# Block-causal attention with a two-stage expert MLP on one Trainium2 core: scores of query blocks 0 to 3 as two rounded full-array products per head

## The chip, the cores and the metric

The kernel runs on one core of one Trainium2 chip. The metric is the device time of one execution in microseconds. The kernel before takes 956.35 us, the median of three runs (955.95 to 956.46).

## What is computed

Attention with a mask by blocks of 64 tokens, then a dense MLP with an ELU between its two matrices, then a soft mixture of eight small experts. Inputs are float32: 8 batches, 8 heads, 576 tokens, head size 64; 4608 tokens of width 512 after attention.

```python
scores = scale * np.matmul(q, k.transpose(0, 1, 3, 2))
scores = np.where(block_i >= block_j, scores, -1000000000.0)
attn = softmax(scores); x = np.matmul(attn, v)      # then (B*S, H*D)
h = x @ w_in; g = np.where(h > 0, h, np.exp(np.minimum(h, 0)) - 1)
x = g @ w_out
logits = x @ phi                                    # 32 slots, 8 experts
slot_out = experts(softmax(logits, 0).T @ x)        # relu(. @ w1[e]) @ w2[e]
return softmax(logits, 1) @ slot_out
```

## The kernel before

**Work and stages.** Two heads of one batch are a pair; there are 32 pairs (`n` = 0 to 31), and 36 tiles of 128 tokens for the MLP. Attention of a batch runs ahead of the tiles that need it, so that from about 200 us to 757 us of the span both run side by side: one pair and 1.125 tiles in some 24 us. Then come the last tiles, then the tail with the experts, whose 32 MB of weights are read in part while the tiles still run.

**Order.** No loop runs on the chip. Each step is entered in a `Plan` with its engines, an assumed duration, what it reads and writes, and a key (a due time); `Plan.order` plays the steps through with those durations and writes the order of every engine. An engine then works through its list strictly in order, so a step that is not ready holds all that stand behind it on that engine. TensorE's steps carry a mode: F (the array as one 128 by 128 block), R (two halves of 64 rows), C (column halves), D (four blocks of 32 columns), and the plan charges 0.13 for a change between them.

**One pair.** `pair_load` brings q and k; `pair_prep` makes q and k transposed (head size on partitions, head 0 on 0 to 63, head 1 on 64 to 127). Pairs 0 to 7 (`n < NTP`) load rows and turn them on TensorE (L360) with ScalarE copies (L521). From pair 8 on, blocks of 32 are loaded and turned by VectorE (L525), and GpSimd scales q (L528, L531). RQ, RK, QT and KT have two buffers each, by `n % 2`. `pair_scores` has four fills: fill 0 is the last half block of queries (block 4, 64 rows, from pair 8 on as a full-array product, L568); fills 1, 2 and 3 are query block 3, blocks 2 and 0, and block 1, for both heads (L576). These are plain float32 products over 64 rows, the two heads on the two halves of the array. Each unit then gets its mask (VectorE memset, L584), its maximum (VectorE, L587) and its exponential with sum (ScalarE, L590). `pair_weights` normalises on GpSimd (L607), turns the result (VectorE L689 and a DRAM round trip `swapped`, TensorE L360 for some blocks), and `swapped_values` multiplies with v (L739, mode C).

**One tile.** `tile_split` rounds x to a high part on ScalarE (L793) and takes the rest on GpSimd (L795). Then, for four ranges of 512 columns, twelve rounded products (L808 to L810, mode F) fill one of two PSUM banks, ScalarE takes the exponential (L813), VectorE clips it (L815, SBUF to SBUF) and takes the maximum with the bank (L818), which frees the bank for the range after next. The result is turned by VectorE (L826) and a DRAM round trip (`turned`); the routing products (L853, L919, mode D) follow, with L880 and L881 between.

**DMA.** Nearly all transfers are issued by SyncE (SP), in one list (L355).

## Time and profile before

| | |
|---|---|
| median of three runs | 956.35 us (955.95 to 956.46) |
| profiled execution, its own time | 955.77 us |
| its span, first to last instruction | 954.0 us |
| TensorE busy / VectorE / ScalarE / GpSimd | 908.7 / 675.9 / 439.4 / 272.6 us |
| granted TensorE clock, mean | 0.99 |

Busy time is what the profiler saw as running; matmuls overlap in it, so that TensorE's real pace is read from the chain of work (each step from the end of the one before), not from the mean length of an instruction. Two records stand for one float32 product and one for a rounded product, so "L576 x4" is two products.

### The profile page before, as it was taken

What the parts mean: (1) busy time and instruction counts of PE and PEld (TensorE: products, weight loads), DVE (VectorE), ACT (ScalarE), POOL (GpSimd) and SP (SyncE); (2) the same over time, 40 slices, a digit from 0 to 9 for tenths busy, and PEclk for the clock granted to TensorE, in tenths of its full rate; (3) what the DMA queues carried; (4) which work ended last, traced back from release to release, by engine and by line L of the source; (5) the groups of instructions that cost most, each with busy time, mean ns of one, the idle gap of its engine ahead of it and who ended that gap; (6) DMA issues with size and microseconds to landing.
All of it is one profiled execution on the core that took longest, in us unless ns stands there. A gap on an engine that the chain in (4) does not pass through costs nothing.

```text
span 954.0 us, 19403 instructions
## 1 busy us (share of the span) xinstructions
PE 908.7 (95%) x6708; PEld 623.3 (65%) x6708; DVE 675.9 (71%) x1718; ACT 439.4 (46%) x1285; POOL 272.6 (29%) x428
## 2 busy tenths in 40 slices
PE   8889999999999999999999999999999999999992
PEld 6556777666666766676766666766776776766350
DVE  5887795668787887777888878887887844333160
ACT  5775655445445535444445445444444333322143
POOL 2863442133342332222323432332332210000000
PEclk9999999999999999999999999999999999999996
DMA  9846755647777785767677777667756498068969
GB/s 235 243 130 171 220 184 159 146 115 207 202 203 218 197 209 184 212 181 211 194 203 206 199 208 201 202 188 203 206 163 217 144 305 340 3 216 298 377 223 342
DMA packets 253217, 197.08 MB, mean 207 GB/s; under 512 B 183232, under 2 KB 206400, under 8 KB 250048
## 3 DMA queue, kind: packets, MB, share of 16 engines
q1 hardware_dynamic: 251920, 195.55, 69.1%
q8 instruction: 54, 0.88, 0.4%
q10 hardware_dynamic: 1200, 0.30, 0.1%
q14 instruction: 43, 0.35, 0.1%
HBM read 125.52 MB, written 70.25 MB: 205 GB/s over the span
## 4 chain that ended last, share of the span: by engine, by line
PE 74%; DVE 8%; DMA 7%; SPq 4%; ACT 2%; issue 2%; POOL 1%; ACTq 0%; DVEq 0%; POOLq 0%
PE ps L808 13%; PE ps L810 11%; PE ps L809 11%; PE ps L360 8%; PE ps L576 7%; PE ps L739 7%; SPq L355 4%; PE ps L919 3%; PE ps L568 2%; PE ps L853 2%; DMA att<-swapped 2%; DMA swapped<-att 2%; PE ps L767 2%; DVE base L587 2%; PE ps L460 1%
## 5 line engine op out<-in xcount | busy, mean ns | idle before, releaser
L808 PE MATMUL ps<-w,xhl 128*128 128x512 f32 x576 | 249.8, 434 | 7.8 <-DVE g L818 5.5
L607 POOL TENSOR_SCALAR att<-att,base 128x128 f32<-128x128 f32 (+4 forms) x288 | 181.0, 647 | 222.2 <-DVE base L603 151.0
L810 PE MATMUL ps<-w,xhl 128*128 128x512 f32 x576 | 226.8, 394 | 0.0
L809 PE MATMUL ps<-w,xhl 128*128 128x512 f32 x576 | 225.7, 392 | 0.0
L590 ACT ACTIVATE att<-ps,base 128x128 f32<-128x128 f32 (+4 forms) x288 | 157.4, 552 | 122.9 <-DVE base L587 121.0
L587 DVE TENSOR_REDUCE base<-ps 128x1 f32<-128x128 f32 (+4 forms) x288 | 135.7, 503 | 21.3 <-PE ps L572 12.2
L808 PEld LDWEIGHTS ps<-w,xhl 128*128 128x128 f32 x576 | 108.8, 189 | 52.0 <-issue 19.1
L813 ACT ACTIVATE xe<-ps 128x512 f32<-128x512 f32 x144 | 86.0, 600 | 115.0 <-PE ps L810 113.7
L810 PEld LDWEIGHTS ps<-w,xhl 128*128 128x128 f32 x576 | 108.1, 188 | 24.9
L336 ACT COPY att<-ps 128x128 f32<-128x128 f32 (+3 forms) x192 | 75.7, 434 | 95.8 <-PE ps L360 90.6
L809 PEld LDWEIGHTS ps<-w,xhl 128*128 128x128 f32 x576 | 108.9, 189 | 14.8
L815 DVE TENSOR_SCALAR xe<-xe 128x512 f32<-128x512 f32 x144 | 68.1, 473 | 67.0 <-ACT xe L813 65.6
L576 PE MATMUL ps<-att 64*128 64x128 f32 (+3 forms) x512 | 96.1, 468 | 1.0 <-ACT att L590 1.0
L360 PE MATMUL ps<-base,att 128*128 128x128 f32 (+1 forms) x496 | 83.2, 282 | 9.7 <-POOL att L607 8.5
L360 PEld LDWEIGHTS ps<-base,att 128*128 128x128 f32 (+1 forms) x496 | 58.0, 143 | 44.5 <-POOL att L607 17.6
L795 POOL TENSOR_TENSOR xhl<-xe,xhl 128x512 fp32r<-128x512 f32 x36 | 46.3, 1291 | 133.1 <-ACT xhl L793 127.0
L818 DVE TENSOR_TENSOR g<-xe,ps 128x512 f32<-128x512 f32 x108 | 73.3, 680 | 2.4
L689 DVE STREAM_TRANSPOSE att<-att 128x384 f32<-128x384 f32 x144 | 70.4, 507 | 5.3 <-POOL att L607 4.2
L739 PE MATMUL ps<-att 128*64 128x64 f32 (+4 forms) x864 | 71.9, 318 | 1.2 <-DMA att<-swapped 0.7
L576 PEld LDWEIGHTS ps<-att 64*128 64x128 f32 x512 | 42.0, 185 | 40.6 <-issue 14.1
L739 PEld LDWEIGHTS ps<-att 128*64 128x64 f32 x864 | 46.8, 137 | 32.3 <-issue 23.6
L826 DVE STREAM_TRANSPOSE g<-g 128x512 f32<-128x512 f32 x84 | 58.0, 695 | 1.7 <-DMA turned<-g 0.2
(134 smaller groups left out, 1115.1 us busy)
## 6 DMA issues: line engine op xcount, KB each, us to landing
turned<-g SPq DMA_DIRECT2D x60, 512.0 KB, 3.1
swapped<-att SPq DMA_DIRECT2D x24, 1024.0 KB, 4.6
g<-turned SPq DMA_DIRECT2D x120, 96.0 KB, 2.6
att<-in_moe_w_dram SPq DMA_DIRECT2D x11, 1024.0 KB, 11.8
att<-swapped SPq DMA_DIRECT2D x48, 192.0 KB, 3.9
att<-in_v_dram SPq DMA_DIRECT2D x64, 128.0 KB, 3.2
g<-in_moe_w_in_dram SPq DMA_DIRECT2D x16, 512.0 KB, 5.3
w_late<-in_moe_w_dram SPq DMA_DIRECT2D x8, 1024.0 KB, 6.9
```

What stands on the lines that cost most here:

```text
L336: nc.scalar.copy(o, i)
L360: mm(o, lhsT=i, rhs=f(IDN + base, n, base, base + n), start=True, stop=True, is_transpose=True)
L576: mm(pb(at((u, h)), P * (u + 1)), lhsT=f(qt + P * u, P, 64 * h, 64 * h + 64), rhs=f(kt, P * (u + 1), 64 * h, 64 * h + 64), start=True, sto ...
L587: add("DVE", 0.08 + wide(x) / 960, lambda e, x=x, c=c: nc.vector.tensor_reduce(out=f(c, 1), in_=pb(at(x), wide(x)), axis=AX.X, op=ALU.max, ...
L590: add("ACT", 0.50 + wide(x) / 1300, lambda e, x=x, c=c: nc.scalar.activation(f(pat(x, n), wide(x)), pb(at(x), wide(x)), AF.Exp, bias=f(c, ...
L607: add("POOL", (0.28 + wide(x) / 1050) * (1.3 if n < 8 else 1.0), lambda e, x=x, p=p: nc.gpsimd.tensor_scalar(out=f(p, wide(x)), in0=f(p, w ...
L739: mm(pb(o, w, 64 * h, 64 * h + 64), lhsT=f(vs + 320 * h + D * c, D), rhs=rhs(h), start=start, stop=stop)
L808: mm(pb(bank, 512), lhsT=fr(xh + P * kk, P), rhs=hi, start=(kk == 0), stop=False)
L809: mm(pb(bank, 512), lhsT=fr(xh + P * kk, P), rhs=lo, start=False, stop=False)
L810: mm(pb(bank, 512), lhsT=fr(xl + P * kk, P), rhs=hi, start=False, stop=(kk == 3))
L813: add("ACT", 0.48, lambda e: nc.scalar.activation(f(ee, 512), pb(bank, 512), AF.Exp), r=[("h", hb)], w=[("e", hb)], key=kr)
L818: add("DVE", 0.6, lambda e: nc.vector.tensor_tensor(out=f(g, 512), in0=f(ee, 512), in1=pb(bank, 512), op=ALU.max), r=[("e", hb), ("h", hb) ...
```

## The change

Pairs 9 to 31 (`n >= STACK`, 23 pairs) compute fills 1 to 3 in another way; pair 8 goes over to the load and preparation of pairs 0 to 7. For a head, q is rounded (`X1`, ScalarE) and its difference taken (`X2`, GpSimd); k likewise (`Y`, `KL`). The rounded q is copied by DMA to the other 64 partitions, and k's difference goes by DMA below the rounded k, so that `X1` holds the high part twice, `Y` the high over the low part, and `X2` the low part over zeros. Two rounded products over all 128 rows, `X1` by `Y` and `X2` by `Y`, are added up in PSUM: high by high, high by low, low by high. `RQ`, `RK`, `QT`, `KT` and the stacks have one buffer for these pairs; q and k of a pair are loaded once the buffer is free, and `pair_prep` is entered behind the scores of the pair before. The masks of fill 2 are two memsets and not four. In the tail, one of the 1 MB weight slots comes in four transfers.

```diff
+TLAG, LATE, NTP, JOINED, STACK = 2.5, 30, 8, 5, 9
-    RQ = aa.take(2 * S)
-    RK = aa.take(2 * S)
-    QT = aa.take(2 * S)
-    KT = aa.take(2 * S)
+    RQ, QB = PT + 8 * XW + 4 * YW, PT + 8 * XW + 4 * YW + S
+    RK = aa.take(S)
+    QT = (aa.take(S), qa.take(S))
+    KT = (aa.take(S), qa.take(S))
...
+    def pair_split(n, key):
+        add("POOL", 0.64, lambda e: nc.gpsimd.tensor_scalar(
+            out=f(QT[0], 512), in0=f(QT[0], 512), scalar1=SCALE, scalar2=0.0, op0=ALU.mult, op1=ALU.add), w=[("qt", 0)], key=key + 0.5)
+        for h in range(2):
+            here, there = (D * h, D * h + D), (D - D * h, P - D * h)
+            x1, x2, y, kl = X1[h], X2[h], Y[h], KL
+            add("ACT", 0.5, lambda e, x1=x1, here=here: nc.scalar.copy(st(x1, 512, *here), f(QT[0], 512, *here)),
+                r=[("qt", 0)], w=key_of(0), key=key + 1)
+            add("ACT", 0.5, lambda e, y=y, here=here: nc.scalar.copy(st(y, 512, *here), f(KT[0], 512, *here)),
+                r=[("kt", 0)], w=key_of(1), key=key + 1)
+            load(lambda x1=x1, there=there: st(x1, 512, *there, F32), lambda x1=x1, here=here: st(x1, 512, *here, F32), 200000,
+                 r=key_of(0), w=key_of(2), key=key + 2, lag=TLAG)
+            add("POOL", 1.35, lambda e, y=y, here=here: nc.gpsimd.tensor_tensor(
+                out=st(KL, 512, *here), in0=f(KT[0], 512, *here), in1=st(y, 512, *here, F32), op=ALU.subtract),
+                r=[("kt", 0)] + key_of(1), w=[("kl", h)], key=key + 2)
+            load(lambda y=y, there=there: st(y, 512, *there, F32), lambda here=here: st(KL, 512, *here, F32), 200000,
+                 r=[("kl", h)], w=key_of(3), key=key + 3, lag=TLAG)
+            add("POOL", 1.47, lambda e, x1=x1, x2=x2, here=here: nc.gpsimd.tensor_tensor(
+                out=st(x2, 512, *here), in0=f(QT[0], 512, *here), in1=st(x1, 512, *here, F32), op=ALU.subtract),
+                r=[("qt", 0)] + key_of(0), w=key_of(4), key=key + 3)
...
+        if n >= STACK and not last:
+            for h in range(2):
+                mine = [u for u, y in units if y == h]
+                def st_sc(e, h=h, mine=mine):
+                    for u in mine:
+                        for x, first in ((X1, True), (X2, False)):
+                            mm(pb(at((u, h)), P * (u + 1)), lhsT=st(x[h] + P * u, P), rhs=st(Y[h], P * (u + 1)), start=first, stop=not first)
+                add("PE", sum(2 * (0.016 + P * (u + 1) / 2400) for u in mine), st_sc, r=[("stack", h, j) for j in range(6)], w=[bkeys[h]], key=key)
...
-        ev.append((base - (27 if n < NTP else KLD), lambda n=n, x=base - KLD: pair_load(n, x)))
-        ev.append((base - 14, lambda n=n, x=base - 14: pair_prep(n, x)))
+        ev.append((base - (27 if n < STACK else KLD) if n < STACK else max(base - KLD, free + 0.1), lambda n=n, x=base - KLD: pair_load(n, x)))
+        ev.append((before + 12.1 if n >= STACK else base - 14, lambda n=n, x=base - 14: pair_prep(n, x)))
```

The plan writes all lists anew. The next fence shows TensorE's list at fill 2 of pair 15 (L576 scores, L808 to L810 the tile's products) before:

```order
L808 MATMUL ps<-w_69,xhl 128x512
L809 MATMUL ps<-w_69,xhl 128x512
L810 MATMUL ps<-w_69,xhl 128x512
L576 MATMUL ps<-att 128x384 x2
L576 MATMUL ps<-att 128x128 x2
L808 MATMUL ps<-w_69,xhl 128x512
L809 MATMUL ps<-w_69,xhl 128x512
L810 MATMUL ps<-w_69,xhl 128x512
```

and now, at the same fill, where L620 is the stacked scores, L854 to L856 the tile's products, L899 and L965 routing, L926 and L927 what were L880 and L881:

```order
L899 MATMUL ps<-g,base 32x128 x16
L965 MATMUL ps<-att,base 32x512 x4
L854 MATMUL ps<-w_71,xhl 128x512
L855 MATMUL ps<-w_71,xhl 128x512
L856 MATMUL ps<-w_71,xhl 128x512
L620 MATMUL ps<-qk_late_2028 128x384 x2
L620 MATMUL ps<-qk_late_2028 128x128 x2
L926 MATMUL ps<-base 128x128
L927 MATMUL ps<-base 128x32
L620 MATMUL ps<-qk_late_2028 128x384 x2
L620 MATMUL ps<-qk_late_2028 128x128 x2
L854 MATMUL ps<-w_68,xhl 128x512
```

The scores now stand in the mode of the work around them, with twice the products, one head after the other, and other work may stand between the heads.

GpSimd's list between two preparations of q (L528 and L531), at pair 15, before:

```order
L528 TENSOR_SCALAR base<-att 64x64 x2
L531 TENSOR_SCALAR att<-att 128x512
L607 TENSOR_SCALAR att<-att,base 128x384 x2
L607 TENSOR_SCALAR att<-att,base 128x128 x2
L607 TENSOR_SCALAR att<-att,base 128x256 x2
L795 TENSOR_TENSOR xhl<-xe,xhl 128x512
L607 TENSOR_SCALAR att<-att,base 128x576
L607 TENSOR_SCALAR att<-att,base 128x512 x2
```

and now (L534 and L546 prepare q, L653 normalises, L841 is the tile's difference, L565 and L560 are the differences of q and k):

```order
L534 TENSOR_SCALAR att<-att 64x64 x2
L546 TENSOR_SCALAR att<-att 128x512
L653 TENSOR_SCALAR att<-att,base 128x576
L653 TENSOR_SCALAR att<-att,base 128x512 x2
L565 TENSOR_TENSOR qk_late_2028<-att,qk_late_2028 64x512
L560 TENSOR_TENSOR qk_late_2028<-att,qk_late_2028 64x512 x2
L565 TENSOR_TENSOR qk_late_2028<-att,qk_late_2028 64x512
L653 TENSOR_SCALAR att<-att,base 128x384 x2
L653 TENSOR_SCALAR att<-att,base 128x128 x2
L653 TENSOR_SCALAR att<-att,base 128x256 x2
L841 TENSOR_TENSOR xhl<-xe,xhl 128x512
```

Four differences in a row now stand ahead of the second half of the normalising.

## Rows read from the trace of the kernel before

**Rows 1.** The page, busy time and share of each engine.
```profile
PE 908.7 (95%) x6708; PEld 623.3 (65%) x6708; DVE 675.9 (71%) x1718; ACT 439.4 (46%) x1285; POOL 272.6 (29%) x428
```
**Rows 2.** Stretch: length; busy us of PE, PEld, DVE, ACT, POOL; granted clock; DMA.
```profile
200.00:757.00 557.00, 547.96 (x3934) 379.42 (x3933) 452.33 (x1200) 258.56 (x826) 177.31 (x303) 1.00 0.70 196
```
**Rows 3.** Waits of TensorE from 200 to 757 us: us, times, longest.
```profile
PE ps L808 <- DVE g L818: 5.5, 6, 2.0
PE ps L808 <- DVE att L818: 2.2, 3, 1.0
```
**Rows 4.** Waits of SP's queue, whole span.
```profile
SPq L1001 <- POOL xhl L795: 40.3, 1, 40.3
```
**Rows 5.** Chain of work in order of time: start us, us, what (records).
```profile
412.21 1.06 PE ps L576 x4
...
415.57 0.23 PE ps L809
...
416.73 0.22 PE ps L880 x2
416.95 0.14 PE ps L881 x2
417.09 1.07 PE ps L576 x8
418.16 0.43 PE ps L808
```
**Rows 6.** The same view at other places of the span.
```profile
163.34 1.12 PE ps L572 x8
...
320.87 0.44 PE ps L360 x4
...
428.63 0.97 PE ps L568 x4
429.61 0.23 PE ps L808
...
450.91 0.63 PE ps L576 x4
451.54 0.59 PE ps L360 x4
```
**Rows 7.** Groups: busy us, mean ns, idle; L795 and L815 from 200 to 757.
```profile
L795 POOL TENSOR_TENSOR xhl<-xe,xhl 128x512 fp32r<-128x512 f32 x27 | 34.7, 1288 | 60.1 <-ACT xhl L793 54.0 <-PE ps L360 6.1
L815 DVE TENSOR_SCALAR xe<-xe 128x512 f32<-128x512 f32 x104 | 49.7, 478 | 24.0 <-ACT xe L813 22.7
L441 ACT CAST w<-g 128x512 fp32r<-128x512 f32 x12 | 7.2, 624 | 1.3 <-DVE g L431 1.3
```
**Rows 8.** DMA issues: count, KB each, median us to landing.
```profile
att<-in_v_dram SPq DMA_DIRECT2D x64, 128.0 KB, 3.2
```
**Rows 9.** Timeline of SP's queue: start us, us, what.
```profile
410.75 2.06 SPq L355 DMA_DIRECT2D att<-in_k_dram  x4
```
**Rows 10.** Lines L815 and L818: duration ns min/median/max.
```profile
L815 DVE TENSOR_SCALAR xe<-xe x144: 373/427/1236, 89.8 to 867.2; 128x512 f32<-128x512 f32 x144
L818 DVE TENSOR_TENSOR g<-xe,ps x108: 643/687/690, 90.7 to 867.6; 128x512 f32<-128x512 f32 x108
```
**Rows 11.** Timelines of GpSimd, VectorE and TensorE: start, us, what, [idle before <-releaser].
```profile
212.64 1.04 DVE L815 TENSOR_SCALAR xe<-xe 128x512 f32<-128x512 f32 x1
...
214.51 0.50 PE L808 MATMUL ps<-w,xhl 128*128 128x512 f32 x1 [1.97 <-DVE g L818]
...
274.12 1.29 POOL L795 TENSOR_TENSOR xhl<-xe,xhl 128x512 fp32r<-128x512 f32 x1 [2.37 <-ACT xhl L793]
...
274.45 1.24 DVE L815 TENSOR_SCALAR xe<-xe 128x512 f32<-128x512 f32 x1
...
276.47 0.50 PE L808 MATMUL ps<-w,xhl 128*128 128x512 f32 x1 [0.85 <-DVE g L818]
...
691.98 0.64 DVE L815 TENSOR_SCALAR xe<-xe 128x512 f32<-128x512 f32 x1 [0.41 <-ACT xe L813]
```

More of the change, by code (lines that the diff above doesn't have):

```diff
@@ L258, in attention_moe_kernel @@
     SM = base.take(144)
-    QB = base.take(2 * P)
     XR = xe.take(4 * RING)
@@ L280, in attention_moe_kernel @@
     PB = aa.take(2 * PW[0] + PW[1])
+    X1, X2, Y, KL = (0, 512), (1024, 1536), (2048, 2560), 3072
+    qa.take(KL + 512 - qa.size)
     XH = xa.take(2 * 512)
@@ L321, in pb, with st @@
         return ps[p0:p1, o:o + n]
+    def st(x, n, p0=0, p1=P, dtype=F32R):
+        t = renew("qk", F32R)
+        return (t if dtype == F32R else t.bitcast(F32))[p0:p1, x:x + n]
     H0, GTB, POST, SB0, PTB, PVB = 0, 1024, 1536, 2048, 3072, 3584
@@ L531, in pair_prep @@
-        add("POOL", 0.55, lambda e: nc.gpsimd.tensor_scalar(
-            out=f(QT + S * s, 512), in0=f(QT + S * s, 512), scalar1=SCALE, scalar2=0.0, op0=ALU.mult, op1=ALU.add),
-            w=[("qt", s)], key=key + 1)
+                out=f(QB + P * s + D * h, D, D * h, D * h + D), in0=f(QT[0] + 512, D, D * h, D * h + D),
+                scalar1=SCALE, scalar2=0.0, op0=ALU.mult, op1=ALU.add), r=[("qt", 0)], w=[("qb", s, h)], key=key + 3.5)
+        if n == STACK:
+            handover([("stack", h, j) for h in range(2) for j in range(6)], [("qt", 1), ("kt", 1)] + [("raw", x, h) for x in range(3) for h in range(3)])
+            for h in range(2):
+                add("POOL", 0.4, lambda e, h=h: nc.gpsimd.memset(st(X2[h], 512, D - D * h, P - D * h, F32), 0.0), w=[("stack", h, 5)], key=key - 20)
@@ L553, in pair_scores @@
         s = n % 2
-        qt, kt = QT + S * s, KT + S * s
+        one = s if n < STACK else 0
+        qt, kt = QT[one], KT[one]
         banks, bkeys = ((H0, H0 + 512), [("h", 0), ("h", 1)]) if n < 4 and fill % 2 else ((SB0, SB0 + 512), [("sb", 0), ("sb", 1)])
@@ L564, in sc @@
         def sc(e):
-            if fill == 0 and n >= NTP:
+            if fill == 0 and n >= STACK:
                 for y in range(2):
@@ L578, in pair_scores @@
         cols = S if fill == 0 else sum(wide(x) for x in units) // 2
-        last = fill == 0 and n >= NTP
-        add("PE", (0.0 if last else 0.15) + cols / 600, sc, r=([("qb", s, 0), ("qb", s, 1)] if last else [("qt", s)]) + [("kt", s)], w=bkeys, key=key,
-            load=1.0, mode="F" if last else "R")
+        last = fill == 0 and n >= STACK
+        if n >= STACK and not last:
+            for h in range(2):
+                mine = [u for u, y in units if y == h]
[4 more added lines that the diff above has]
+                add("PE", sum(2 * (0.016 + P * (u + 1) / 2400) for u in mine), st_sc, r=[("stack", h, j) for j in range(6)], w=[bkeys[h]], key=key)
+        else:
+            add("PE", (0.0 if last else 0.15) + cols / 600, sc, r=([("qb", s, h) for h in range(3)] if last else [("qt", one)]) + [("kt", one)],
+                w=bkeys, key=key, load=1.0, mode="F" if last else "R")
         for x in units:
-            if x != "b":
+            if n >= STACK and fill == 2 and x[0] == 2:
+                both = pb(at(x) + 256, 256, 0, 64).rearrange("p (a y) -> p a y", a=2)[:, :, 64:]
+                add("DVE", 0.14, lambda e, both=both: nc.vector.memset(both, MASKED), w=keys(x), key=key)
+            elif x != "b" and not (n >= STACK and fill == 2):
                 add("DVE", 0.11, lambda e, x=x: nc.vector.memset(pb(at(x) + P * x[0] + 64, 64, 0, 64), MASKED), w=keys(x), key=key)
@@ L985, in tail, with __getitem__ @@
         wslot = [(held("w%d" % r, j), wk[r]) for r in range(4) for j in range(2)]
-        slots = [(flat(PT + PIECE * j), att) for j in range(10)]
+        class Parted:
+            def __getitem__(self, at):
+                c = at[1]
+                t = renew("qk", F32, 1)[:, PIECE + 512 * c:PIECE + 512 * c + 512] if c < 3 else f(PT + 8 * PIECE, 512)
+                return t
+        parted = Parted()
+        slots = [(flat(PT + PIECE * j), att) for j in range(8)]
+        slots += [(lambda: renew("qk", F32, 1)[:, 0:PIECE].rearrange("p (c d) -> p c d", d=512), qkk), (lambda: parted, qkk + att)]
         slots += [(flat(TT), tgk(0, 0) + tgk(0, 1))]
@@ L1000, in fn @@
                 o = at()
-                nc.sync.dma_start(out=o.rearrange("p (c f) d -> p c (f d)", f=2) if wide else o,
-                                  in_=src.rearrange("(c p) d -> p c d", p=P))
-            add("SP", 0.48, fn, r, pkeys(j), kp, 1 << 20)
+                if o is not parted:
+                    nc.sync.dma_start(out=o.rearrange("p (c f) d -> p c (f d)", f=2) if wide else o,
+                                      in_=src.rearrange("(c p) d -> p c d", p=P))
+                    return
+                for c in range(4):
+                    part = src[P * (c // 2):P * (c // 2) + P, 512 * (c % 2):512 * (c % 2) + 512] if wide else src[P * c:P * c + P, :]
+                    nc.sync.dma_start(out=o[:, c, :], in_=part)
+            add("SP", 0.48 if j != 9 else 1.9, fn, r, pkeys(j), kp, 1 << 20)
             return at, j
@@ L1177, in attention_moe_kernel @@
     ev = []
+    before = None
     for n in range(NPAIR):
```

50 lines of the change are left out of this document (27 added, 23 removed).

## Prediction

> **What bounds the kernel now.** I read the page first: TensorE is busy for 95% of the span, VectorE for 71% [rows 1]. An average over stages can mislead, so the next view is the stretch that the change touches, 200 to 757 us, in which pairs and tiles run side by side. There TensorE is busy for 548.0 of 557.0 us at the full clock (1.00, that is 2.4 GHz), VectorE for 452.3, GpSimd for 177.3 [rows 2]. So 9 us of TensorE's time are open, and its waits say whose they are: 5.5 and 2.2 us before a tile's first product L808, until VectorE's L818 has freed the PSUM bank [rows 3]. TensorE's own list of work bounds this stretch; VectorE is second. What TensorE saves here comes off the end nearly in full, as long as no new wait takes its place. The tail shifts as a whole: SP's queue stands 40.3 us before the tail's weights because slots are still held by the last tiles [rows 4], so an earlier end of the tiles lets the weights start earlier by as much.
>
> The sum is made against the profiled execution: 954.0 us of span, 955.8 of its own time, 0.6 below the median of the runs.
>
> **The products.** Pace is read from the chain. Fills 1, 2 and 3 now take 1.06, 1.07 and 0.63 us [rows 5, 6]; 23 pairs make 23 x 2.76 = 63.5 us. After the change a pair has 16 rounded products: four each of 512, 384, 256 and 128 columns. A rounded full-array product of 512 columns takes 0.23 in the chain (L809) [rows 5]. For narrow ones two rows bound the pace: L881, only 32 columns wide but with full weight loads, takes 0.14 for two records, 0.07 each [rows 5], and a 128-column transpose takes 0.44 for four, 0.11 each [rows 6]. I take 0.23, 0.18, 0.12 and 0.08: 4 x 0.61 = 2.44 us a pair, 56.1 in all, a gain of **7.4 us**. With plain proportion to the width it is 2.30 (gain 10.6), with 0.11 at the narrow end 2.56 (gain 4.6). So the gain on the products alone is small.
>
> **The changes of mode.** The other half is what follows a half-array block. L808 right behind L576 takes 0.43 [rows 5], behind L568 0.23 [rows 6]; four transposes behind L576 take 0.59, else 0.44 [rows 6]. A return to the whole array costs 0.15 to 0.20 us, taken as 0.19. In TensorE's list I counted the returns from modes R, C and D to F: 150 before (87 from R, 15 from C, 48 from D), 107 now (28, 25, 54). A part of what R gave up is paid by C and D blocks that used to share a return with R. So 43 x 0.19 = **8.2 us**. The entry into R is inside the 63.5 already.
>
> **Pair 8** goes back to ten transposes on TensorE (10 x 0.11 = 1.1) and its fill 0 from 0.97 to 1.12 plus a return [rows 6]: **1.5 us** against. Its four ScalarE copies lie beside other work.
>
> TensorE's list is thus shorter by 7.4 + 8.2 - 1.5 = **14.1 us** (11 to 17.5 with the bounds above).
>
> **What hides the rest, and what if not.** Per pair, ScalarE gets four casts, at most 0.62 us each (L441, on twice the partitions) [rows 7], GpSimd four differences at some 1.29 (L795) [rows 7], SP four issues of some 0.5 [rows 9]. In sum 57, 119 and 46 us, against 298, 380 and much of SP's time free in the stretch [rows 2]; taken at nothing as sums. VectorE loses two memsets a pair, and pair 8's two transposes: at nothing too, a gain of 1 us at the most, since VectorE's stalls are 7.7 us in all [rows 3]. Three places are not covered by sums.
>
> First, **GpSimd against VectorE**. At 274.12 a tile's difference L795 starts on GpSimd and runs to 275.41; L815 starts on VectorE at 274.45 and takes 1.24 us, to 275.69, where its median is 0.427 and its maximum 1.236; L818 follows, and TensorE's L808 waits 0.85 [rows 10, 11]. The same stands at 212.64, before the longest wait of the stretch, 1.97 [rows 11]. Of the 27 L795 in the stretch [rows 7], six lie over the start of an L815 (first 212.64, second 274.45, last 691.98 [rows 11]); these six lose 2.6 us together, of which I trace 1.8 to waits of TensorE (0.6 of the 1.97, 0.8 of the 0.85, and 0.4 at two short waits of L880 for VectorE). The change adds 92 instructions of L795's kind: 92 x 1.8 / 27 = **6.1 us** lost. Below: nothing, if they fall where L815 does not stand on the path. Above: 104 L815 in 557 us [rows 7] and 119 us of differences give 22 meetings; at the worst one seen, 0.81 us, and all of it passed on, 18 us. The value taken is nearest to the rows, being the same instruction by count.
> The Trainium skill's page "SBUF — State Buffer", section "Who interferes with whom", states that GpSimd shares one port pair with VectorE as an exclusive lock, and that a VectorE `tensor_scalar` in a two-port mode waits until a running GpSimd instruction has ended. By that rule the mean wait would be half of 1.29, 0.65 us, and 22 x 0.65 = 14 us of VectorE time, if every meeting holds. The trace agrees with the lock at 274.45, and with the other side of the Trainium skill's rule too, that an instruction with one SBUF and one PSUM input goes free: L818 stays within 643 to 690 ns [rows 10].
>
> Second, **the stack comes late**. With one buffer, nothing of the next pair's stack can be written before fill 3 of the pair is done. Then four casts (the first must end before a difference starts), three differences up to the second head's k, an issue and a 128 KB transfer (v's takes 3.2 us [rows 8]): 0.62 + 3 x 1.29 + 0.5 + 3.2 = 8.2 us. In the new list I added up TensorE's work between fill 3 and the next fill 1 with the chain's durations: 22 gaps, mostly 9.3 to 13.3 us, three short ones of 6.0, 7.1 and 7.8. The first head's fill 1 (0.46) may run first, so 1.7 and 0.6: **2.3 us** lost. At nothing if the chain is under 6.5 us; the upper end is a rival below. Queued behind a late transfer on SP are the `turned` loads that feed the routing products, and behind the differences on GpSimd the second half of the normalising.
>
> Third, ScalarE has four casts, 2.5 us, ahead of the exponential L813 of the bank that was just filled. The two banks cover 12 x 0.23 = 2.8 us, and L813, L815 and L818 need about 1.7; the cover is 1.1. I take nothing, with 5 us (0.2 a pair) as the upper end.
>
> **Sum.** 955.8 - 14.1 + 6.1 + 2.3 = 950.1; plus 0.6 to the median, 950.7. Forecast **950.7 us**.
>
> **The rivals.** (a) *The gain comes whole.* The meetings fall where VectorE has room, and the stack is early. For it: three short gaps only, and most of TensorE's gaps exceed 9 us. Against it: two of the longest waits already come from such meetings. 956.35 - 14.1 = 942; with the upper end of the products 939. (b) *GpSimd's lock eats it all.* A new wait of L808 for L818 takes the place of what was saved: 13 to 16 us, that is most of the 22 meetings at 0.65 us passed on; 955 to 958. For it speaks the lock as the Trainium skill states it (SBUF page, above); against it that the six meetings of before passed on two thirds of 2.6 us, and that tiles mostly have other work between two ranges. (c) *Slower: the stack is late at fill 1.* Place: TensorE at L620 with 512 columns, in order, so everything behind it stands. With the 22 gaps, a chain of 9.5 us costs 8 us, of 10.5 us 13, of 11 us 17, of 12 us 29. With the lock's 6.1 paid, it decides from about 9.5 us on: only 1.3 over my 8.2, which holds no hops and no queueing. At 11 us the time is 956.35 - 14.1 + 6.1 + 17 = 965. Against it: the transfer lies inside the core and may land in less than v's 3.2, and later waits overlap with it. (d) *The change does not do what it says*: rounded products are paced by their weight loads at 0.19 or more whatever the width, 73.6 us for 23 pairs, a loss of 10 where 7.4 were gained; 968. L881 at 0.07 a record speaks against it.
>
> **How the numbers follow.** Forecast 0.48 (own range 946 to 954.4), (a) 0.23, (b) 0.12, (c) 0.13, (d) 0.04. What a measurement of this kernel can tell from no change is about 0.2%, 954.4 to 958.3. Faster: the forecast and (a), 0.71; same: (b), 0.12; slower: (c) and (d), 0.17. The range goes from 940, inside (a), to 962, the lighter half of (c).
>
> **What would show it.** In the changed profile: L620 at 0.23, 0.18, 0.12, 0.08 in the chain, and L854 behind it at 0.23; TensorE's list shorter by about 14 us; waits of L854 for VectorE's L864 of some 14 us where 7.7 stood, with L861 long under an L560 or L565; waits of L620 for a DMA or GpSimd of 2 to 3 us, at three pairs. The forecast is wrong if L620 waits at most pairs, if narrow L620 take 0.19, or if TensorE's waits stay at 9 us (then a).

## The result: slower by 1.4%

The changed kernel takes 969.13 us (median; 966.05 to 970.76), the kernel before 956.15 in the runs beside it: ratio 1.0138, 95% interval 1.0105 to 1.0170. The forecast was 950.7 with a range of 940 to 962, so it missed the side and the range. The profiled execution of the changed kernel took 968.08 us, its span is 966.3. One of the four executions of a later run, e2, took 2224 us and is left out of its time.

| | before | after |
|---|---|---|
| median, us | 956.15 | 969.13 |
| span of the profiled execution, us | 954.0 | 966.3 |
| whole span: TensorE busy / idle, us | 908.7 / 45.3 | 908.3 / 58.0 |
| 200 to 757 us: TensorE busy / open, us | 547.96 / 9.0 | 536.48 / 20.5 |
| the same: VectorE, ScalarE, GpSimd busy, us | 452, 259, 177 | 461, 314, 295 |
| the same: granted clock, DMA share | 1.00, 0.70 | 0.99, 0.79 |

"Open" is the stretch of 557 us less TensorE's busy time, "idle" the same of the whole span. The stretch has the same length in every kernel, so a slower kernel gets less of its work done in it, and its busy and open time mirror each other; how long the work itself takes is read from the whole span, in which every kernel does all of it. First the page's busy times of the changed kernel and the row of the stretch (length; busy us of PE, PEld, DVE, ACT, POOL; granted clock; DMA share; GB/s); they answer to [rows 1, 2].

```profile
PE 908.3 (94%) x6721; PEld 654.2 (68%) x6721; DVE 687.5 (71%) x1656; ACT 501.4 (52%) x1396; POOL 390.3 (40%) x519
...
200.00:757.00 557.00, 536.48 (x3870) 402.28 (x3869) 460.96 (x1122) 314.42 (x918) 294.76 (x396) 0.99 0.79 216
```

TensorE's and VectorE's shares of the page have hardly moved. TensorE is busy over the whole span for as long as before (908.3 against 908.7 us), and the 12.3 us by which the span grew are idle time. Its waits over the whole span (us, times, longest), which answer to [rows 3]:

```profile
PE ps L854 <- DVE g L864: 6.8, 6, 2.7
PE ps L854 <- DVE att L864: 5.7, 4, 2.1
PE ps L1161 <- DMA qk_late<-in_moe_w_dram: 2.6, 1, 2.6
PE ps L899 <- DMA g<-turned: 1.8, 1, 1.8
...
PE ps L620 <- ACT att L636: 1.4, 3, 0.6
...
PE ps L620 <- DMA qk_late<-qk_late: 0.5, 1, 0.5
```

L854 is what L808 was, L864 what L818 was. A tile's first product waits 12.5 us for its bank, where it waited 7.7: 4.8 us more. The wait for the stack (L620 behind a copy) is 0.5 us. L1161 stands in the tail. Next the chain of work at a place with stacked products (start us, us, what), which answers to [rows 5]:

```profile
221.90 0.91 PE ps L620 x4
222.80 0.23 PE ps L854
...
401.90 0.47 PE ps L620 x4
402.36 0.23 PE ps L854
...
514.71 0.60 PE ps L620 x4
515.32 0.28 PE ps L854
```

Four records of 512 columns take 0.91 us, two of 384 with two of 128 take 0.60, four of 256 take 0.47. A pair needs 0.91 + 2 x 0.60 + 0.47 in these places, some 2.6 us with the step from the narrow ones included; over all records I get medians of 0.23, 0.18, 0.12 and 0.06 to 0.11, and 2.45 us a pair. The tile behind them takes 0.23 to 0.28, not 0.43. So these steps did become shorter, as the prediction says. Yet the busy time of the whole span did not fall by 14.1 us but by 0.4, because other steps became dearer: the first step behind a wait takes 0.50 where 0.23 is normal (0.80 at half the clock, see the last section), and steps at half the clock 0.43. In my count over all records, which sets a step behind a wait or at half the clock against the usual step of its kind, these cost 11.5 us more than usual steps before and 18.9 now. Without that the list is 7.8 us shorter.

### The profile page after: what moved, and what is told of

Its sections match the earlier page's. It is cut to its first block, busy times and chain, and to the rows that moved or that the text cites. A ratio compares the mean times of both kernels' runs of the same rounds, so it can differ in the third digit from the quotient of the medians.

```text
span 966.3 us, 19890 instructions
## 1 busy us (share of the span) xinstructions
PE 908.3 (94%) x6721; PEld 654.2 (68%) x6721; DVE 687.5 (71%) x1656; ACT 501.4 (52%) x1396; POOL 390.3 (40%) x519
## 4 chain that ended last, share of the span: by engine, by line
PE 64%; DVE 12%; DMA 9%; ACT 4%; SPq 3%; POOL 3%; issue 2%; ACTq 0%; DVEq 0%; POOLq 0%
PE ps L854 11%; PE ps L856 10%; PE ps L855 9%; PE ps L367 7%; PE ps L785 6%; PE ps L620 4%; SPq L362 3%; PE ps L965 3%; PE ps L899 2%; DVE base L633 2%; POOL att L653 2%; DMA att<-swapped 2%; PE ps L609 2%; PE ps L601 1%; ACT att L636 1%
## 5 line engine op out<-in xcount | busy, mean ns | idle before, releaser
L653 POOL TENSOR_SCALAR att<-att,base 128x128 f32<-128x128 f32 (+4 forms) x288 | 181.5, 647 | 202.8 <-DVE base L649 141.2
L854 PE MATMUL ps<-w,xhl 128*128 128x512 f32 x576 | 250.5, 435 | 12.9 <-DVE g L864 6.8
L856 PE MATMUL ps<-w,xhl 128*128 128x512 f32 x576 | 227.9, 396 | 0.0
L633 DVE TENSOR_REDUCE base<-ps 128x1 f32<-128x128 f32 (+4 forms) x288 | 137.7, 502 | 21.1 <-PE ps L605 11.1
L854 PEld LDWEIGHTS ps<-w,xhl 128*128 128x128 f32 x576 | 109.8, 191 | 51.2 <-issue 13.1
L856 PEld LDWEIGHTS ps<-w,xhl 128*128 128x128 f32 x576 | 108.9, 189 | 25.3 <-POOL xhl L841 0.2
L343 ACT COPY att<-ps 128x128 f32<-128x128 f32 (+3 forms) x202 | 78.5, 430 | 79.9 <-PE ps L367 74.4
L861 DVE TENSOR_SCALAR xe<-xe 128x512 f32<-128x512 f32 x144 | 80.9, 562 | 53.2 <-ACT xe L859 51.7
L565 POOL TENSOR_TENSOR qk_late<-att,qk_late 64x512 fp32r<-64x512 f32 x46 | 61.0, 1325 | 87.0 <-ACT qk_late L554 51.7
L841 POOL TENSOR_TENSOR xhl<-xe,xhl 128x512 fp32r<-128x512 f32 x36 | 46.6, 1294 | 99.4 <-ACT xhl L839 92.4
L620 PE MATMUL ps<-qk_late 128*128 128x512 f32 (+3 forms) x368 | 77.6, 327 | 1.9 <-ACT att L636 1.4
L367 PE MATMUL ps<-base,att 128*128 128x128 f32 x416 | 68.9, 279 | 10.8 <-POOL att L653 9.7
L620 PEld LDWEIGHTS ps<-qk_late 128*128 128x128 f32 x368 | 62.7, 189 | 20.0 <-ACT att L636 8.2
L864 DVE TENSOR_TENSOR g<-xe,ps 128x512 f32<-128x512 f32 x108 | 73.0, 677 | 1.8
L367 PEld LDWEIGHTS ps<-base,att 128*128 128x128 f32 x416 | 49.3, 142 | 35.4 <-POOL att L653 17.4
L785 PE MATMUL ps<-att 128*64 128x64 f32 (+4 forms) x864 | 71.5, 318 | 1.0 <-DMA att<-swapped 0.8
L785 PEld LDWEIGHTS ps<-att 128*64 128x64 f32 x864 | 46.7, 137 | 30.9 <-issue 23.8
```

The lines of the kernel that those rows point to most:

```text
L343: nc.scalar.copy(o, i)
L367: mm(o, lhsT=i, rhs=f(IDN + base, n, base, base + n), start=True, stop=True, is_transpose=True)
L620: mm(pb(at((u, h)), P * (u + 1)), lhsT=st(x[h] + P * u, P), rhs=st(Y[h], P * (u + 1)), start=first, stop=not first)
L633: add("DVE", 0.08 + wide(x) / 960, lambda e, x=x, c=c: nc.vector.tensor_reduce(out=f(c, 1), in_=pb(at(x), wide(x)), axis=AX.X, op=ALU.max, ...
L653: add("POOL", (0.28 + wide(x) / 1050) * (1.3 if n < 8 else 1.0), lambda e, x=x, p=p: nc.gpsimd.tensor_scalar(out=f(p, wide(x)), in0=f(p, w ...
L785: mm(pb(o, w, 64 * h, 64 * h + 64), lhsT=f(vs + 320 * h + D * c, D), rhs=rhs(h), start=start, stop=stop)
```

## The experiments

All times are medians; the kernel before ran beside each group and took 955.0 to 957.2 us. A ratio in brackets is to it. Differences between runs of different groups can be off by some 2 us for that reason. The trace has 92 subtractions and 92 casts, those of pairs 9 to 31; where the expectations say 108 and pairs 9 to 35, these are meant.

### One piece of the splitting at a time, the order kept

The planner writes each engine's list from assumed durations. In e1 to e5 these assumptions stay as in the changed kernel, so that every list keeps its order and only what an entry emits is different; e6 moves entries of VectorE's list alone.

**e1_diff8** (subtractions on 8 of 512 columns):

```diff
-  out=st(KL, 512, *here), in0=f(KT[0], 512, *here), in1=st(y, 512, *here, F32), op=ALU.subtract
+  out=st(KL, 8, *here), in0=f(KT[0], 8, *here), in1=st(y, 8, *here, F32), op=ALU.subtract
   (the same for X2; KL and X2 set to zero once, at pair 9)
```

> The changed kernel (969.1 us) with each of the 108 subtractions on GpSimd done on 8 of its 512 columns; the other columns of the low parts stay zero (set once), so the low halves of the products are left out. The order of every engine's list, the copies and the products stay. Theory A (subtractions hold VectorE off; VectorE lost 31.7 us to GpSimd in the changed kernel's trace against 8.0 before, and TensorE's waits for the maxima grew by some 18 us): most of that goes, 954 to 960 us, and the mean of the clip L861 falls from 562 ns back to about 473. Theory B (VectorE's list itself: the masks of fill 3 stand ahead of the clip and wait for products that come late): 966 to 969 us. Theory C (the stack comes late: TensorE waits at L620, 2.4 us in all): 965 to 967 us.

Measured: 965.2 us (1.0094, 1.0079 to 1.0109), so 3.9 us given back, where theory A wanted 9 to 15. (The waits that theory A puts at some 18 us had grown by 4.8 in the whole span, from 7.7 to 12.5.) The lock itself is plain in the trace. First of the changed kernel, around the longest wait of TensorE in the stretch, the timeline of GpSimd, VectorE and TensorE (start us, us, what, [idle before <-releaser]):

```profile
326.51 2.60 POOL L560 TENSOR_TENSOR qk_late<-att,qk_late 64x512 fp32r<-64x512 f32 x2
329.07 1.26 POOL L565 TENSOR_TENSOR qk_late<-att,qk_late 64x512 fp32r<-64x512 f32 x1
...
327.93 1.21 DVE L648 TENSOR_SCALAR base<-base 128x6 f32<-128x6 f32 x1 [1.69 <-ACT att L636]
...
329.29 1.34 DVE L861 TENSOR_SCALAR xe<-xe 128x512 f32<-128x512 f32 x1
330.66 0.69 DVE L864 TENSOR_TENSOR g<-xe,ps 128x512 f32<-128x512 f32 x1
...
331.40 0.80 PE L854 MATMUL ps<-w,xhl 128*128 128x512 f32 x1 [2.67 <-DVE g L864]
```

Three subtractions follow one another from 326.51 to 330.33; L648, an addition on six columns, ends at 329.14, just after the second; the clip L861 behind it ends at 330.63, 0.3 us after the third. Now the groups of the stretch (count | busy us, mean ns | idle before), the first two of the changed kernel:

```profile
L861 DVE TENSOR_SCALAR xe<-xe 128x512 f32<-128x512 f32 x102 | 62.1, 609 | 10.1 <-ACT xe L859 8.8 <-issue 0.2
...
L648 DVE TENSOR_SCALAR base<-base 128x6 f32<-128x6 f32 x23 | 16.2, 705 | 9.4 <-ACT att L636 9.2
```

and the same two of e1:

```profile
L861 DVE TENSOR_SCALAR xe<-xe 128x512 f32<-128x512 f32 x102 | 47.8, 468 | 19.9 <-ACT xe L859 18.2 <-issue 0.2
...
L648 DVE TENSOR_SCALAR base<-base 128x6 f32<-128x6 f32 x23 | 3.8, 166 | 10.3 <-ACT att L636 10.2
```

In these two lines alone the lock costs VectorE 14.3 + 12.4 = 26.7 us. The Trainium skill's page "SBUF — State Buffer", section "Who interferes with whom", has this as an exclusive lock; the trace agrees, and shows it on six columns as on 512. Of the 26.7 us, 3.9 reach the end: without the lock VectorE waits instead (L861's idle time rises from 10.1 to 19.9 us). In the profiled executions TensorE's idle time over the whole span does not fall either, it is 60.5 us against 58.0; what falls is its busy time, from 908.3 to 902.7, and with it the steps at half the clock (the granted clock of the stretch is 1.00 in e1 and 0.99 in the changed kernel). Theory A falls as the main cause.

**e2_diff_quarters** (each subtraction in four of 128 columns):

```diff
-  nc.gpsimd.tensor_tensor(out=st(KL, 512, *here), in0=f(KT[0], 512, *here), in1=st(y, 512, *here, F32), ...)
+  [nc.gpsimd.tensor_tensor(out=st(KL + 128 * i, 128, *here), in0=f(KT[0] + 128 * i, 128, *here), ...) for i in range(4)]
```

> The changed kernel with each subtraction cut into four of 128 columns each; nothing else moves. If what costs is the longest single hold of VectorE (1.3 us, or 2.6 where two follow each other), VectorE gets in between the pieces and the time falls by 3 to 8 us, to 961 to 966. If what costs is the total time held, or the order of the list, the time stays at 968 to 972 (the pieces add some fixed cost to GpSimd).

Measured: 975.4 us (1.0208). Worse by 6 us, though the holds did become milder. The groups of e2's stretch, and what VectorE's transpose of the next q (L531) waits for, first in the changed kernel, then in e2:

```profile
L861 DVE TENSOR_SCALAR xe<-xe 128x512 f32<-128x512 f32 x101 | 51.5, 510 | 7.7 <-ACT xe L859 7.0
L648 DVE TENSOR_SCALAR base<-base 128x6 f32<-128x6 f32 x23 | 6.9, 300 | 9.4 <-ACT att L636 9.1
...
DVE att L531 <- POOL qk_late L565: 3.4, 5, 1.1
...
DVE att L531 <- POOL qk_late L565: 21.1, 14, 3.7
```

VectorE gets 19.9 of its 26.7 us back. But the quarters take GpSimd 162 us in the stretch where the whole subtractions took 121, and with one buffer the next q can't be turned before they are done: that wait grows by 17.7 us. That this wait makes the 6 us is likely, not shown.

**e3_cast8** (casts L554 and L556 on 8 columns):

```diff
-  nc.scalar.copy(st(x1, 512, *here), f(QT[0], 512, *here))
+  nc.scalar.copy(st(x1, 8, *here), f(QT[0], 8, *here))
   (the same for Y; X1 and Y set to zero once, at pair 9)
```

> The changed kernel with each of the 108 casts on ScalarE done on 8 of its 512 columns (the rest of the high parts stays zero, set once, so most of the products' data is left out); subtractions, copies, products and order stay. Theory C (casts delay the exponentials and the stack): 960 to 966 us. Theories A and B (VectorE): 967 to 969 us, since ScalarE is busy 52% and is waited for in no more than 2 us of TensorE's idle time.

Measured: 966.6 us (1.0106), 2.5 us given back, between the ranges of theory C and of theories A and B. Its four runs (964.7 to 967.6) overlap those of the changed kernel (966.1 to 970.8), so that a price of the casts is not clear of the scatter.

**e4_plain**:

```diff
-  for u in mine:
-      for x, first in ((X1, True), (X2, False)):
-          mm(pb(at((u, h)), P * (u + 1)), lhsT=st(x[h] + P * u, P), rhs=st(Y[h], P * (u + 1)), ...)
+  for u, y in (units if h == 0 else ()):
+      mm(pb(at((u, y)), P * (u + 1)), lhsT=f(qt + P * u, P, 64 * y, 64 * y + 64), ...)
```

> The changed kernel with fills 1 to 3 of pairs 9 to 35 computed by the old plain row-tiled products (both heads at the place of the first), while all of the splitting (casts, subtractions, copies) still runs, unused. By the terms of the prediction (products 7.4, returns to full-array mode 8.2 us) TensorE's list grows by about 14 us: 981 to 984 us if TensorE's list sets the end. If waits set the end and the list has slack, 969 to 974 us.

Measured: 995.0 us (1.0412), 26 us more, where 12 to 15 were expected. TensorE goes back to the whole array 131 times behind 213 us instead of 75 (counted over all records), 56 x 0.2 = 11 us, and the products take 74 us where the stacked ones take 63, both with their waits. The 26 us are no price of the stacked products: the order was planned for those, and e4 leaves out the wait of the second head's products for a bank of their own. The run shows that plain products are no better in this place, and not by how much.

### All of the load, VectorE's order, the layout alone

**e5_all8** (the edits of e1 and e3, and the copies):

```diff
-  load(lambda x1=x1, there=there: st(x1, 512, *there, F32), lambda x1=x1, here=here: st(x1, 512, *here, F32), ...)
+  load(lambda x1=x1, there=there: st(x1, 8, *there, F32), lambda x1=x1, here=here: st(x1, 8, *here, F32), ...)
   (the same for the copy of KL to Y)
```

> The changed kernel with casts, subtractions and copies alike on 8 of 512 columns (the rest of the stack stays zero, so most of the products' data is left out); every engine's order and the products stay. The subtractions alone gave back 4 us (965.2), the casts alone 2.5 (966.6). If the load that the splitting puts on ScalarE, GpSimd and the queues is what eats the gain, all of it together gives 945 to 955. If the order of the lists (fixed here) is what eats it, the time stays at 960 to 965 and TensorE's idle time over 0.3 us stays near 20 us, where the kernel before has 9.

Measured: 959.5 us (1.0023, 0.9998 to 1.0049). The splitting load costs 9.6 us in this order; 3.9 and 2.5 are the parts run alone, the other 3.2 belong to the copies or to the parts together, which was not run apart. But the products that are now almost free of load give no gain either, and TensorE is idle for 54.2 us of the span where it was 45.3 before. Neither expectation holds fully: the load explains the loss against 956, not the missing 14. One load stays whole in e5: each of the 92 copies moves 8 columns, but SP still issues it.

**e6_yield** (score masks and maxima go behind a tile's clip and maximum where they stood directly ahead):

```diff
+  if e == "DVE" and i in self.late:      # masks L628, L630 and maxima L633
+      held.append((t, i, e, j))
+      continue
+  if held and (e == "DVE" and i not in self.first or i >= 0 and self.ops[i][3] & {x[1] for x in held}):
+      out += held; held = []             # first: L861, L864
```

> The changed kernel, complete, with one thing moved: where the masks or maxima of the scores stand in VectorE's list directly ahead of a tile's clip L861 or maximum L864, the clip and the maximum go first; nothing else moves on any engine. If masks that wait for late products hold the clip up (the waits of 1.39, 1.60 and 1.72 us of L854 at 521, 544 and 570 us), those three shrink by half or more and the time falls by 2 to 5 us, to 964 to 967. If not, 968 to 970.

Measured: 970.6 us (1.0139), no gain. Its waits of TensorE (17 lines lower than in the changed kernel: L871 is L854, L637 is L620, L802 is L785):

```profile
PE ps L871 <- DVE att L881: 4.4, 5, 2.4
PE ps L871 <- DVE g L881: 4.2, 4, 2.7
PE ps L637 <- ACT att L653: 3.2, 5, 1.5
PE ps L802 <- DMA g<-turned: 2.8, 3, 1.3
```

The wait for the tile's bank fell from 12.5 to 8.6 us, and the score products now wait 3.2 us for the exponentials (1.4 in the changed kernel): the wait changed its place. The three waits of L854 at 521, 544 and 570 us that the run aimed at shrank to 0.65, 0.45 and 0.18 us; one of 2.0 us behind ScalarE stands at 557 now, and the time is the same.

**e7_layout** (no splitting, plain products, `pair_split` left with the scaling alone):

```diff
-  if n >= STACK and not last:
+  if False:
```

> The changed kernel's layout without its products: one buffer instead of two for the transposed q and k of pairs 9 to 35, pair 8 by way of TensorE, loads and preparation at the new times; fills 1 to 3 are the old plain row-tiled products and nothing is split. If the layout (the single buffer, pair 8, the new order that follows) is what eats the gain, 963 to 972. If the layout is harmless, 956 to 959 (pair 8 adds 1.5 us).

Measured: 966.4 us (1.0092, 1.0065 to 1.0118). The layout, in the order planned for it, loses 10 us with the old products. But e7 is also the first run whose lists are another draw of the planner. What a new draw costs had to be measured.

### The kernel before, its work untouched, in other orders

```diff
n1  -CHANGE, STAY, JOIN = 0.13, 0.0, 0.0      +CHANGE, STAY, JOIN = 0.16, 0.0, 0.0
n2  -add("DVE", 0.335, ...clip...)             +add("DVE", 0.36, ...clip...)
n3  -NTP, JOINED = 2.5, 30, 8, 5               +NTP, JOINED = 2.5, 30, 9, 5
n5  -CHANGE, STAY, JOIN = 0.13, 0.0, 0.0      +CHANGE, STAY, JOIN = 0.10, 0.0, 0.0
```

> The kernel before, complete, with one number of the planner changed: it assumes 0.16 us for a change of TensorE's mode instead of 0.13. No instruction is added or removed; the lists of all engines come out in another order (about 740 lines of TensorE's list move, as many as under the change). Theory D (the list order of the kernel before is a lucky one, and any replanning costs TensorE idle time): 960 to 968 us. Theory L (what the layout run lost came from its single buffers and pair 8): 955 to 958 us.

> The kernel before, complete, with another number of the planner changed: it assumes 0.36 us for the clip on VectorE instead of 0.335. A second draw of the same kind. Theory D: 960 to 968 us. Theory L: 955 to 958 us.

> The kernel before with pair 8 alone moved to the way of pairs 0 to 7 (q and k transposed on TensorE, fill 0 as half-array products); both buffers of q and k stay. By the prediction's term this adds 1.5 us to TensorE's list: 957 to 959 us if pair 8 is all there is; by theory D, being replanned too, 960 to 968; if the single buffers are what the layout run lost, 957 to 959 as well.

> The kernel before, complete, with the planner's price of a mode change at 0.10 us instead of 0.13: a third draw of a replanned list. Theory D: 960 to 968 us. Theory L: 955 to 958 us.

Measured: n1 951.2 (0.9948, 0.9933 to 0.9963), n2 965.3 (1.0090), n3 963.8 (1.0078), n5 962.4 us (1.0067). (n3 does not get all values right, for a cause that stays open; nothing below rests on it.) Both theories are half wrong: replanning costs 6 to 9 us in two draws and gains 5 in a third, by chance better than both kernels of the case. The stretch of n1, to be held against [rows 2]:

```profile
200.00:757.00 557.00, 552.29 (x3987) 382.00 (x3985) 453.19 (x1205) 261.62 (x826) 178.64 (x308) 1.00 0.69 196
```

TensorE is open for 4.7 us here, 12.6 in n2 and 14.1 in n5, with the same work; over the whole span it is idle for 40.2, 49.6 and 49.7 us. Order alone moves this kernel by 14 us.

### The changed kernel in other orders

```diff
c1  -CHANGE, STAY, JOIN = 0.13, 0.0, 0.0      +CHANGE, STAY, JOIN = 0.16, 0.0, 0.0
c2  -add("DVE", 0.335, ...clip...)             +add("DVE", 0.36, ...clip...)
c3  -CHANGE, STAY, JOIN = 0.13, 0.0, 0.0      +CHANGE, STAY, JOIN = 0.10, 0.0, 0.0
c4  -add("DVE", 0.335, ...clip...)             +add("DVE", 0.43, ...clip...)
```

> The changed kernel, complete, replanned with 0.16 us for a change of mode (0.13 before). Theory D (the changed kernel got an unlucky order; the change itself is worth what the prediction's terms say, about -6): the draws c1 to c4 scatter as widely as those of the kernel before (951 to 965) around 953, so 946 to 960. Theory X (the splitting costs TensorE its gain and more in any order): all draws at 965 to 973. In between (the change is neutral by itself): around 959.

> The changed kernel, complete, replanned with 0.36 us for the clip L861 (0.335 before). Theory D: 946 to 960. Theory X: 965 to 973. Neutral: around 959.

> The changed kernel, complete, replanned with 0.10 us for a change of mode. Theory D: 946 to 960. Theory X: 965 to 973. Neutral: around 959.

> The changed kernel, complete, replanned with 0.43 us for the clip L861, its measured median in the stretch. Theory D: 946 to 960. Theory X: 965 to 973. Neutral: around 959. If a truer length of the clip makes a better list, this is the fastest of the four.

Measured: c1 967.0 (1.0128), c2 974.1 (1.0197), c3 966.5 (1.0114), c4 966.4 us (1.0126). Theory X, with c2 1 us above its range: five of five draws lie at 966 to 974, and not one gets down to the slowest of the old work (965.3). The truer length of the clip in c4 is no better than c3. The first order of the changed kernel was not unlucky.

### A ladder under the same planner numbers

```diff
f1  the edits of e5_all8 and   -CHANGE, STAY, JOIN = 0.13, 0.0, 0.0   +CHANGE, STAY, JOIN = 0.16, 0.0, 0.0
f2  the edits of e5_all8 and   -CHANGE, STAY, JOIN = 0.13, 0.0, 0.0   +CHANGE, STAY, JOIN = 0.10, 0.0, 0.0
f3  the edits of e7_layout and -CHANGE, STAY, JOIN = 0.13, 0.0, 0.0   +CHANGE, STAY, JOIN = 0.16, 0.0, 0.0
```

> c1 (967.0 us) with casts, subtractions and copies on 8 of 512 columns; its order is kept, the rest of the stack stays zero, so most of the products' data is left out. If the splitting load costs what it cost in the first order (9.6 us), 956 to 959; if that was the first order's luck, 962 to 967. Against n1 (951.2), the same planner number without the change: if the stacked products gain 14 us in any order, as predicted, 937 to 942; if the single buffers and the waits that follow take that back, 951 to 960.

> c3 (966.5 us) treated in the same way (most of the products' data left out, order kept). Splitting load as in the first order: 955 to 959. No load effect: 963 to 967. Against n5 (962.4): products' gain whole, 948 to 951; gain partly taken back, 953 to 960.

> The layout run (old plain products, nothing split, single buffers for q and k, pair 8 by TensorE) replanned with 0.16 us for a change of mode. Against n1 (951.2): if the layout costs what it seemed to cost in its first order (some 8 to 10 us), 959 to 962; if that was the order's luck and only pair 8 counts, 951 to 955; the scatter of replanning is some 5 us either way.

Measured: f1 960.6 (1.0057), f2 956.4 (1.0017), f3 958.4 us (1.0035). f1 and f3 lie between the ranges that were expected, f2 where the load costs as much as in the first order. With the runs above, median us, and in brackets TensorE's idle time over the whole span of the profiled execution; "8 columns" are the stacked products with casts, subtractions and copies cut to 8 of 512 columns, all of them still issued:

| planner number | old work | layout alone | stacked, 8 columns | whole change |
|---|---|---|---|---|
| mode change 0.13 | 956.2 (45.3) | 966.4 (51.6) | 959.5 (54.2) | 969.1 (58.0) |
| mode change 0.16 | 951.2 (40.2) | 958.4 (44.0) | 960.6 (53.2) | 967.0 (55.6) |
| mode change 0.10 | 962.4 (49.7) | | 956.4 (51.1) | 966.5 (57.1) |
| clip 0.36 | 965.3 (49.6) | | | 974.1 (62.3) |
| clip 0.43 | | | | 966.4 (59.4) |

Two steps can be read. **From 8 columns to the whole change**: 9.6, 6.5 and 10.1 us, 8.7 in the mean; the order of the lists is the same on both sides, and the three lie within 4 us. **From the old work to stacked products on 8 columns**: 3.3, 9.4 and -5.9 us, 2.3 in the mean, where the prediction had -14. Here the order differs on the two sides, and the layout and SP's issues are in it too. The three scatter by the planner's draw, but none comes near -14. The layout's step is 10.2 and 7.2 us, two draws only.

So where did the gain go? The pages of the pair with 0.16, n1 and f1:

```profile
span 949.3 us, 19434 instructions
PE 909.1 (96%) x6717; PEld 623.5 (66%) x6717; DVE 677.2 (71%) x1719; ACT 442.0 (47%) x1284; POOL 267.6 (28%) x428
...
span 958.5 us, 19892 instructions
PE 905.3 (94%) x6731; PEld 654.3 (68%) x6731; DVE 667.5 (70%) x1670; ACT 460.6 (48%) x1380; POOL 290.3 (30%) x527
```

On 8 columns TensorE's busy time falls by 5.5, 3.8 and 4.7 us in the three orders, and its idle time grows by 8.9, 13.0 and 1.4. In the count that sets dear steps against usual ones, the list itself is 9.8, 11.3 and 14.2 us shorter; 4 to 10 us of this go to dearer steps behind waits and at half the clock, and the rest, or more, to the waits. TensorE's waits in f1's stretch:

```profile
PE ps L785 <- DMA att<-swapped: 7.5, 5, 3.4
PE ps L854 <- DVE att L864: 4.3, 4, 1.9
PE ps L899 <- DMA g<-turned: 1.7, 3, 1.1
...
PE ps L785 <- DMA g<-turned: 1.1, 2, 0.8
```

The products of the probabilities with v (L785) wait for the transposed probabilities to land; the same wait in the stretch of the kernel before was 0.2 us. The longest, 3.4 us, in SP's queue (start us, us, what):

```profile
465.94 2.21 SPq L362 DMA_DIRECT2D att<-in_q_dram  x4
468.25 2.61 SPq L362 DMA_DIRECT2D att<-in_k_dram  x3
470.90 3.08 SPq L362 DMA_DIRECT2D att<-swapped  x6
```

and in the chain:

```profile
473.10 0.43 SPq L362
473.52 0.04 issue
473.57 3.53 DMA att<-swapped
477.10 0.04 issue
477.14 4.39 PE ps L785 x32
```

Loads of the next pair's q and k stand ahead of the six loads that TensorE needs. The write that these six read back had landed at 465.24; the last of them is issued at 473.57 and lands 3.53 us later. At eleven other waits of this kind of 0.9 us or more (three more in f1, two in f2, six in c1 to c4) it is the same: the write had landed 4 to 8 us before the last of the six is issued, some 3 us of which the six take themselves, and SP issues without a break just before them. Over all draws TensorE's waits for a landing transfer in the stretch, 0 to 0.9 us with the old work, are 0.8 and 4.1 in the layout's, 3.5, 11.1 and 7.5 on 8 columns, and 3.3 to 6.0 in the five of the whole change. From the old work to 8 columns they grow by 2.9, 11.1 and 7.2 us, while the waits for VectorE change by +2.1, +1.8 and -6.3. The stack's copies add 92 issues to SP in the stretch:

```profile
L362 SPq DMA_DIRECT2D qk_late<-qk_late x92: 461/500/1968, 214.0 to 746.2; - x92
```

(duration ns min/median/max). SP's issues take 378 us of the 557 before and 457 after (751 and 846 of them, counted over all records). In e5, f1 and f2 all of these issues are still there (856 to 865 of them), so that the middle column of the table is not free of load for SP. What the time would be without them is open: no run took the copies out of SP's list, moved the loads to another queue or changed their order there, and none gave the stacked kernel its second buffer back.

## Why the prediction was wrong, point by point

- **Products, -7.4: held, step by step.** The stacked ones take 0.23, 0.18, 0.12 and 0.06 to 0.11 us, 2.45 a pair, against 2.44 taken. Rival (d), narrow products paced by their weights, fell.
- **Returns to the whole array, -8.2: held.** Behind 213 us the records show 120 before and 75 after, 45 x 0.2 = 9 us.
- **"What TensorE saves here comes off the end nearly in full": this step failed.** Counted in usual steps, the list of the stacked products on 8 columns is 9.8, 11.3 and 14.2 us shorter in three orders, near the 14.1 of the forecast. The time changed by +3.3, +9.4 and -5.9 us. The saving went into waits (TensorE's idle time +8.9, +13.0 and +1.4 us) and into dearer steps behind them and at half the clock. The new waits that the prediction made its condition ("as long as no new wait takes its place") did come, on 8 columns most of them for transfers, a place that it did not price. The 9 us that were open in one trace were read as proof that the list bounds the stretch. They were the outcome of one order: with the same work the idle time of the span runs from 40.2 to 49.7 us, and the time from 951 to 965. VectorE is busy for 81% of the stretch before, SP's issues take 68% of it, and each list is in order; so a shorter TensorE list can meet the next late thing, in these traces the bank behind L864 and the transfers behind SP. That is read from the waits; no run eased SP's queue.
- **GpSimd's lock, +6.1 (0 to 18): the lock is there, the size near, the way not.** 3.9 us by e1. The way there was wrong on both counts: VectorE lost 26.7 us in two lines, not the 92 x 2.6 / 27 = 9 that the six meetings of before give, and a seventh of it reached the end, not two thirds. L648, the six-column addition ahead of the reciprocal, was not in the prediction at all and took nearly half of the loss. In the profiled executions what reached the end did so as steps at half the clock and not as idle time. Rival (b), the lock eating all of the gain, fell with e1.
- **The late stack, +2.3: not seen as such.** L620 waits 0.5 us for a copy. Rival (c), which put the loss at this place, had the right sign by the wrong mechanism.
- **ScalarE's casts, 0 (up to 5): 2.5** by e3, not clear of the scatter. The prediction's own rows left 2.5 - 1.1 = 1.4 us of a pair's casts uncovered, and it gave no reason for taking nothing.
- **SP's issues, at nothing as a sum of 46 us: mis-sized.** 92 copies at the median 0.50 us are 46, but all issues in the stretch grew by 79 us, and SP's queue stands on TensorE's path at the longest wait of f1.
- **All of the splitting, 6.1 + 2.3 = 8.4: 8.7** measured in the mean of three orders. The total was right by luck: its parts were not, and SP's issues are on both sides of what was measured.
- **Left out: the layout and the new draw.** One buffer for q and k in place of two was priced only through the stack. By e7 and f3 it loses 10 and 7 us with the old products, inside the scatter of a draw but with the same sign twice. And a planner's new order was treated as neutral, where it moves this kernel by up to 14 us; the range of 940 to 962 holds nothing for that.
- **Half clock: not in the prediction.** See the last section.
- Sum, from 956.2: stacked products, layout, SP's issues and draw together +3.3 where -14.1 stood, load +9.6 where +8.4 stood: 969.1.

What stays open: why TensorE is idle for 1 to 13 us more with the stacked products on 8 columns than with the old work, 8 in the mean. SP's 92 more issues, the single buffer of q and k and the draw of the order are all in that step, and no run takes them apart. The waits shift between the bank (L854) and the transfers (L785, L899) from draw to draw, and neither e6 nor e1 could remove them by easing one place.

## What to carry to other kernels

Before a shorter list on the busiest engine is booked as a gain, replan the old work two or three times with a harmless number changed: the scatter is the floor of what a prediction can claim, and the idle time in the good and the bad draw shows how far that engine's list is the bound. Compare idle and busy time over the whole span: a window of fixed length holds less of the work of the slower kernel. Fix the order and take pieces of the change away (here 6.5 to 10.1 us three times) rather than compare two different orders, and look which load the piece leaves behind (here SP's issues). The best kernel of the study, n1 at 951.2 us, came from a planner's number and not from the change.

## What the runs showed of the hardware

Behind some of its waits TensorE goes on at half its clock. Behind the 2.67 us of idle time at 331.40 the chain of the changed kernel reads:

```profile
331.40 0.80 PE ps L854
332.20 0.43 PE ps L855
332.62 0.43 PE ps L856
...
334.33 0.43 PE ps L854
334.76 0.23 PE ps L855
```

Steps of 0.43 us, where 0.23 is normal: 1.2 GHz in place of 2.4. The row of that stretch has the granted clock at 0.72:

```profile
330.00:336.00 6.00, 4.60 (x14) 3.69 (x15) 5.59 (x10) 0.88 (x3) 4.55 (x8) 0.72 0.78 240
```

Here 2.67 us of waiting cost some 1.5 us more (0.80 where a first step behind a wait takes 0.50, and six of 0.43 for 0.23). The same stands behind waits of 2.08 us at 251 and 1.80 us at 624 (granted clock 0.67 and 0.66 in the five microseconds from there). But not behind every wait: 1.60 and 1.72 us at 544 and 570 were followed by the full clock, as was the longest wait of before, 1.97 us [rows 11]. c2, the slowest draw, shows both: steps at half clock behind waits of 3.31, 2.17, 2.41 and 2.96 us at 216, 260, 478 and 725, and the full clock behind another wait of 2.96 us at 532. Its chain and row there:

```profile
532.14 0.50 PE ps L854
532.64 0.23 PE ps L855
...
532.00:536.00 4.00, 3.86 (x17) 3.21 (x18) 4.00 (x8) 1.32 (x3) 2.13 (x5) 1.00 0.61 218
```

So a wait can be dearer than its length, and its length alone does not tell whether it is.

The lock between GpSimd and VectorE holds whole instructions in a row: six columns on VectorE (0.16 us) took 1.21 us under two subtractions on 64 partitions. And four subtractions of 128 columns take GpSimd some 1.8 us (162 us over 91 of them) where one of 512 takes 1.3, and the kernel is slower with them (975.4 against 969.1 us), although VectorE loses less.
